# Head pairs in attention: keys and values as 64-row halves in place of a zero-padded block diagonal, with two buffers for the strided values

## The chip, the cores and the metric

The kernel runs on one core of a Trainium2 chip. A core has five engines that run their own instruction streams and meet through semaphores: PE (TensorE, matmuls; its weight loads are listed apart as PEld), DVE (VectorE), ACT (ScalarE), POOL (GpSimd) and SP, which here only issues transfers (DMAs). Matmuls write to PSUM, which has eight banks of 512 f32 values in each of 128 partitions; everything else lives in SBUF, which has 128 partitions (rows) too. The metric is the device time of one execution in microseconds, and the median of several runs counts.

## The reference

An attention layer with 8 heads of 64 values over 8 sequences of 576 positions, and behind it a layer in which each of the 4608 tokens goes to one of 8 experts. The change touches the attention alone.

```python
def _attn_ref(q, k, v):
    B, H, S, D = q.shape                       # 8, 8, 576, 64
    scores = np.matmul(q, k.transpose(0, 1, 3, 2)) / np.sqrt(D)
    rel = pos[:, None] - pos[None, :]
    mask_local = (rel >= 0) & (rel < 32)
    mask_strided = (rel >= 0) & (pos[None, :] % 32 == pos[:, None] % 32)
    masks = np.stack([mask_local if h < H // 2 else mask_strided for h in range(H)], axis=0)
    scores = np.where(masks[None, :, :, :], scores, -1000000000.0)
    scores = scores - np.max(scores, axis=-1, keepdims=True)
    attn = np.exp(scores)
    attn = attn / (np.sum(attn, axis=-1, keepdims=True) + 1e-09)
    return np.matmul(attn, v)

x = attention.transpose(0, 2, 1, 3).reshape(4608, 512)
# per token: e = argmax(x @ w_gate); y = relu(x @ w1[e]) @ w2[e], scaled by two gates
```

Four heads are local (a query sees the 32 positions up to itself), four are strided (it sees the earlier positions of its residue modulo 32).

## The kernel before

**Pairs.** Heads are worked on in pairs: `i` counts the two pairs of a kind, `h` the two heads of a pair. Head `h` of a pair holds its 64 values of depth on rows `64h` to `64h + 63`, so one transfer of queries fills 128 rows with two heads (`q_t`). A query block of one pair is then the 128-row stationary operand of one matmul. So that the two heads don't mix, the moving operand is a block diagonal: the key tiles `kbs` (strided) and `kbl` (local) have an extra dimension `h`, and head `h`'s keys stand on its own 64 rows at place `h`, with zeros on the other 64 rows. One matmul of `scores` gives 64 scores of head 0 and 64 of head 1 beside each other. The value tiles `vlt` (local), `vev` (local, shifted by half a block) and `vst` (strided) are block diagonals in the same way, and one matmul of `values` gives 2 x 65 columns (64 values and a column of ones that sums the weights). The zeros are written once by `clear`, at the program's start, by DVE, POOL and ACT. Each half is loaded by a transfer of its own over 64 partitions (`load_s`, `load_l`, `load_v`); of `vst`, which holds three residues of 18 positions per block, 54 of 64 rows are loaded after the first time.

**Query blocks.** `tiles(j, w)` lists what is computed side by side in one 128-row output: four local blocks of 32 queries, or two strided blocks of 64. A sequence has ten such outputs, two (`w`) in each of five steps `j`: `j` = 0 and 1 are all strided, 2 is mixed, 3 and 4 are all local. A step has 8 (strided), 10 (mixed) or 16 (local) matmuls in `scores` and as many in `values`. Every f32 matmul stands in the trace as two matmul records and two weight loads, so these are groups of 16, 20 and 32 records.

**The pipeline.** The order is written out by hand: a loop over `t` = 0 to 39 (`b = t // 5`, `j = t % 5`), and in each pass parts of several steps: `scores(t)`; the three parts of `norm(t - 4)`; `turn_p(t - 2)` (transposes of the weights, PE); `bar(t)` (mask added, DVE); `evac_p(t - 2)` (ACT); `values(t - 3)` (PE); `top(t)` (row maxima, DVE); `shift(t)` (POOL); `expo(t)` (ACT); `turn_x(t - 4)` (PE); and between them, by `pump`, pieces of the routing of an earlier sequence. Each engine works its stream in this order. The output of `scores` is one bank of PSUM out of two buffers (`ps_s`, `bufs=2`); that of `values` is two banks, one buffer.

**SP's queue.** All loads and the 16 stores of a sequence's rows (`rows`) are issued by SP in program order: among the stores come, at `j` = 1, the strided values of the sequence at work (`vst`, one buffer); at `j` = 2 the strided queries and keys of the next sequence; at `j` = 3 its local queries, keys and values (two buffers each). A transfer is given one of eight semaphores in turn, and SP waits until the earlier transfer of the same semaphore has landed. `vst` can be loaded only when `values` of step `j` = 2 of the sequence before has read it, which runs at `j` = 0; it is needed by `values` of step 0, which runs at `j` = 3.

**Behind the attention** the last sequence is routed, its tokens are sorted into a table in DRAM, and `experts` gathers and multiplies. The first of its work for expert 0 (`lead_layer`) fills the last steps of the attention and uses `scores`' PSUM buffers.

Of the kernel before, what the change touches and what calls it, by code (L numbers as in the profile page):

```python
# [7 lines left out]
F32 = mybir.dt.float32  # L8
# [4 lines left out]
ALU = mybir.AluOpType  # L13
# [10 lines left out]
FC = FF // 128  # L24
# [30 lines left out]
def attn_moe_kernel(  # L55
# [106 lines left out]
    def attention():  # L162
        with ExitStack() as actx:
# [7 lines left out]
            ps_s = actx.enter_context(tc.tile_pool(name="ps_s", bufs=2, space=PSUM))  # L171
# [10 lines left out]
            def clear(t, spare=False):  # L182
                if spare:
                    for ps, h in ((slice(0, D), 1), (slice(D, 128), 0)):
                        dims = " ".join("abcd"[:len(t.shape) - 2])
                        o = t[ps, h].rearrange(f"p {dims} -> p ({dims})")
                        nc.scalar.copy(out=o, in_=zeros[ps, 0:1].to_broadcast([D, o.shape[1]]))
                else:
                    nc.vector.memset(t[0:D, 1], 0.0)
                    nc.gpsimd.memset(t[D:128, 0], 0.0)  # L190
                if t in kbl:
                    nc.vector.memset(t[0:D, 0, :, 0, HS:HS + 32], 0.0)
                    nc.gpsimd.memset(t[D:128, 1, :, 0, HS:HS + 32], 0.0)
                if t is vev:
                    nc.vector.memset(t[32:D, 0, 0], 0.0)
                    nc.gpsimd.memset(t[D + 32:128, 1, 0], 0.0)
# [3 lines left out]
            def load_s(b, cs=slice(0, WS)):  # L200
                if b not in qts:
                    qts[b] = inp.tile([128, 4, WS], F32, name="q_t")
                nc.sync.dma_start(out=qts[b][:, srd, cs], in_=qs[b, :, :, cs])
                for h in range(2):
                    hp = slice(D * h, D * (h + 1))
                    nc.sync.dma_start(out=kbs[b % 2][hp, h, :, cs], in_=ks[b, hp, :, cs])

            def load_l(b, c0=0, c1=HS):
                nc.sync.dma_start(out=qts[b][:, loc, 2 * c0:2 * c1], in_=ql[b, :, :, 2 * c0:2 * c1])
                for h in range(2):  # L210
                    hp = slice(D * h, D * (h + 1))
                    nc.sync.dma_start(out=kbl[b % 2][hp, h, :, :, c0:c1], in_=kl[b, hp, :, :, c0:c1])
# [10 lines left out]
            def load_v(b, t, src, n):  # L223
                for h in range(2):
                    nc.sync.dma_start(out=t[D * h:D * h + n, h], in_=src[b, D * h:D * h + n])

            def even(b, eng, h, f):
# [3 lines left out]
                copy(out=vev[ps, h, f:NL].rearrange("p n i e -> p (n i e)"),  # L231
                     in_=vlt[b % 2][ps, h, 0:NL - f].rearrange("p n i e -> p (n i e)"))
# [13 lines left out]
            def query(b, i, m, n):  # L246
                return qts[b][:, i, 32 * n:32 * (n + 1)] if m == 32 else qts[b][:, 2 + i, col0(n):col0(n) + m]

            def keys(b, i, m, n):

                if m == 64:
                    return kbs[b % 2][:, :, i, col0(n):col0(n) + 64]
                e = n // 2
                step = (HS + 32 if n % 2 else HS) // 32
                kb = kbl[b % 2][:, :, i].rearrange("p h f (n k) -> p h (f n) k", k=32)
# [754 lines left out]
```

## Time and profile before

| | |
|---|---|
| median of 3 runs | 720.11 us (719.47 to 724.35) |
| the profiled execution | 726.38 us, of which its span is 724.7 us |
| PE busy | 671.4 us (93%) |
| DVE, ACT, POOL busy | 310.6, 272.0, 193.6 us |
| mean granted TensorE clock | 0.959 |
| from the first instruction to the first of `scores` | 6.1 us |
| `scores` of `t` = 5 begins | at 26.41 us |
| `scores` of `t` = 39 begins | at 208.74 us |
| the expert layer's long run of matmuls | from 262 us to the end |

The times in the table and in the rows further down are microseconds from the span's start. "Busy" is the time in which at least one instruction of the engine runs; matmuls overlap each other, and their ends are modelled, so the step from the first matmul of one group to the first of the next is the better measure of what a group costs. A wait is named by what released it. The granted clock is the share of full speed that PE was given, and the DMA share is the mean busy share of the core's 16 DMA engines.

### The profile page before, as it was taken

The numbers are of one execution on the slowest core, as the hardware profiler recorded it, in microseconds if no ns is written. First come the engines' busy times: TensorE is split into PE (matmuls) and PEld (weight loads), VectorE is DVE, ScalarE is ACT, GpSimd is POOL, SyncE is SP. The second block draws the span as 40 slices with busy tenths as digits, with TensorE's granted clock in tenths as the row PEclk, the third lists the DMA queues.
The fourth block names the chain that finished last, engine by engine and source line by source line (L and its number), as shares of the span: only waits on it lengthen the run. The fifth ranks groups of instructions, "written<-read, shape, count | busy, mean of one in ns | idle before, by whom it ended". The sixth has DMA issues, their size and how long they took to land.

```text
span 724.7 us, 13154 instructions
## 1 busy us (share of the span) xinstructions
PE 671.4 (93%) x5109; PEld 552.3 (76%) x5109; DVE 310.6 (43%) x670; ACT 272.0 (38%) x491; POOL 193.6 (27%) x197
## 2 busy tenths in 40 slices
PE   7978987988866889999999999999999999999995
PEld 4656655656644678889879987988987997997984
DVE  3766755757643552334223331423543433442410
ACT  6544543544342342333323233423423433432420
POOL 4323452454542343140113012101401302301001
PEclk9999988989998989999999999999999999999998
DMA  8896697687932226362144123424514514531001
GB/s 210 216 228 186 160 212 167 159 214 207 218 100 68 96 69 211 108 192 95 64 142 139 59 102 101 145 72 130 167 35 137 166 56 129 161 101 59 15 13 38
DMA packets 46099, 93.22 MB, mean 129 GB/s; under 512 B 8218, under 2 KB 23066, under 8 KB 46036
## 3 DMA queue, kind: packets, MB, share of 16 engines
q1 hardware_dynamic: 36868, 69.44, 35.7%
q0 software_dynamic: 8048, 19.78, 8.1%
q10 hardware_dynamic: 1120, 3.15, 1.2%
q8 instruction: 41, 0.67, 0.4%
q14 instruction: 22, 0.18, 0.1%
HBM read 73.19 MB, written 20.00 MB: 129 GB/s over the span
## 4 chain that ended last, share of the span: by engine, by line
PE 43%; issue 19%; POOL 3%; DMA 1%; POOLq 0%
PE yp L782 21%; PE hp L766 20%; POOL out_dram L799 2%; PE tp L756 2%; POOL xg L147 1%; DMA xg<-xd,tab 1%; POOL table L554 0%; POOLq L799 0%; POOLq L884 0%; POOLq L147 0%
## 5 line engine op out<-in xcount | busy, mean ns | idle before, releaser
L766 PE MATMUL hp<-xh,w1l 128*128 128x256 f32 (+1 forms) x480 | 147.9, 308 | 0.0
L766 PE MATMUL hp<-xl,w1h 128*128 128x256 f32 (+1 forms) x480 | 147.8, 308 | 0.0
L766 PE MATMUL hp<-xh,w1h 128*128 128x256 f32 (+1 forms) x480 | 147.7, 308 | 0.0
L799 POOL DMA_INDIRECT out_dram<-ys,tab x40 | 41.9, 1048 | 353.2 <-ACT ys L798 341.9
L766 PEld LDWEIGHTS hp<-xh,w1h 128*128 128x128 f32 x480 | 91.0, 190 | 2.1
L766 PEld LDWEIGHTS hp<-xl,w1h 128*128 128x128 f32 x480 | 91.0, 190 | 1.9
L766 PEld LDWEIGHTS hp<-xh,w1l 128*128 128x128 f32 x480 | 90.9, 189 | 1.4
L782 PE MATMUL yp<-w2h,hhb 128*128 128x512 f32 (+3 forms) x208 | 83.8, 403 | 0.0
L782 PE MATMUL yp<-w2l,hhb 128*128 128x512 f32 (+3 forms) x208 | 82.2, 395 | 0.0
L782 PE MATMUL yp<-w2h,hlb 128*128 128x512 f32 (+3 forms) x208 | 81.7, 393 | 0.0
L285 POOL TENSOR_TENSOR p_t<-p_t,st 128x512 f32<-128x512 f32 x40 | 48.1, 1203 | 115.0 <-DVE st L281 73.8
L704 DVE TENSOR_TENSOR xl<-tp,xh 128x512 fp32r<-128x512 f32 (+3 forms) x40 | 25.8, 650 | 118.3 <-ACT xh L703 118.3
L770 DVE SCALAR_TENSOR_TENSOR hlb<-hp,hhb 128x480 fp32r<-128x480 f32 (+7 forms) x64 | 34.6, 541 | 85.7 <-ACT hhb L769 72.7
L703 ACT CAST xh<-tp 128x512 fp32r<-128x512 f32 (+3 forms) x40 | 21.9, 555 | 127.9 <-PE tp L756 127.9
L769 ACT ACTIVATE hhb<-hp 128x480 fp32r<-128x480 f32 (+7 forms) x64 | 30.6, 478 | 101.6 <-PE hp L766 92.1
L314 PE MATMUL xp<-vst,pt 128*64 128x130 f32 x352 | 35.4, 322 | 23.5 <-DMA vst<-in_vs_dram 19.2
L782 PE MATMUL yp<-w2h,hha 128*128 128x512 f32 x128 | 51.9, 405 | 2.3 <-ACT w2h L703 2.3
L782 PE MATMUL yp<-w2l,hha 128*128 128x512 f32 x128 | 51.6, 403 | 0.5 <-DVE w2l L704 0.5
L147 POOL DMA_INDIRECT xg<-xd,tab x40 | 46.6, 1166 | 19.3 <-issue 17.7
L554 POOL DMA_INDIRECT table<-meta,dst x48 | 44.3, 923 | 27.5 <-issue 11.5
L782 PE MATMUL yp<-w2h,hla 128*128 128x512 f32 x128 | 51.1, 399 | 0.0
L314 PEld LDWEIGHTS xp<-vst,pt 128*64 128x64 f32 x352 | 24.6, 157 | 31.3 <-issue 30.3
(148 smaller groups left out, 1110.6 us busy)
## 6 DMA issues: line engine op xcount, KB each, us to landing
raw<-in_moe_w_dram SPq DMA_DIRECT2D x54, 512.0 KB
vlt<-in_vl_dram SPq DMA_DIRECT2D x16, 292.5 KB
q_t<-in_ql_dram SPq DMA_DIRECT2D x8, 576.0 KB
kbl<-in_kl_dram SPq DMA_DIRECT2D x16, 288.0 KB
xd<-x_t SPq DMA_DIRECT2D x80, 54.0 KB
vst<-in_vs_dram SPq DMA_DIRECT2D x14, 301.6 KB
q_t<-in_qs_dram SPq DMA_DIRECT2D x7, 586.0 KB
kbs<-in_ks_dram SPq DMA_DIRECT2D x14, 293.0 KB
```

The source lines that it names most:

```text
L147: nc.gpsimd.indirect_dma_start(out=dst, out_offset=None, in_=src, in_offset=bass.IndirectOffsetOnAxis(ap=idx, axis=0), bounds_check=top, o ...
L285: nc.gpsimd.tensor_tensor(out=p_[b, j], in0=p_[b, j], in1=sp_.pop((b, j)).unsqueeze(3).to_broadcast([128, 2, 4, 64]), op=ALU.subtract)
L314: nc.tensor.matmul(out=xp[p0:p0 + m, w, 130 * i:130 * (i + 1)], lhsT=pt[:, w, i, p0:p0 + m], rhs=value(b, i, m, n), start=True, stop=True)
L554: i = nc.gpsimd.indirect_dma_start(out=table[:, :], out_offset=bass.IndirectOffsetOnAxis(ap=dst[:, j:j + 1], axis=0), in_=meta[:, b * NB + ...
L703: nc.scalar.copy(out=hi, in_=src)
L704: nc.vector.tensor_tensor(out=lo, in0=src, in1=f32(hi), op=ALU.subtract)
L756: nc.tensor.transpose(out=tv[:, k, 0:m], in_=xg[0:m, 128 * k:128 * (k + 1)], identity=ident[0:m, 0:m])
L766: nc.tensor.matmul(out=hp[:, 0:n], lhsT=w[:, k, 128 * j:128 * (j + 1)], rhs=x[:, k, 0:n], start=first, stop=(k == KC - 1 and w is w1l))
L769: nc.scalar.activation(out=hh[:, j, 0:n], in_=hp[:, 0:n], func=AF.Relu)
L770: nc.vector.scalar_tensor_tensor(out=hl[:, j, 0:n], in0=hp[:, 0:n], scalar=0.0, in1=f32(hh[:, j, 0:n]), op0=ALU.max, op1=ALU.subtract)
L782: nc.tensor.matmul(out=yp[0:m, :], lhsT=h[:, j, o:o + m], rhs=w[:, j, :], start=(j == 0 and q == 0), stop=(j == FC - 1 and q == 2))
L799: i = nc.gpsimd.indirect_dma_start(out=out[:, :], out_offset=bass.IndirectOffsetOnAxis(ap=tab[:, 0:1], axis=0), in_=ys[0:m, :], in_offset= ...
```

## The change

The block diagonals go. Keys and values lose the dimension `h` and stand on 128 rows as they come from DRAM, each kind loaded by one transfer over 128 partitions. A matmul now takes 64 rows, the upper or the lower half, of queries and keys (or of weights and values): twice as many matmuls, each with half the rows and half the columns (64 in place of 128, 65 in place of 130). The two heads of a pair come one behind the other and write to different PSUM banks: the tile `sp` of `scores` now has two banks, one for each `h`, and one buffer in place of two (`bufs=1`); in `xp` of `values` the two banks, before one for each `w`, are now one for each `h`. `bar` and `norm` read this other arrangement and write the old one; in the mixed step `bar` is two instructions, since the two `w` have different masks. `vst` has two buffers, and the next sequence's strided values are loaded at `j` = 1, whole (64 rows), in place of those of the sequence at work. The local keys come padded from DRAM (320 in place of 288 columns for each parity), so no zeros are written but 2 x 32 rows of one block of `vev`. `lead_layer` takes one tile of two banks and uses its halves in turn.

```diff
-            ps_s = actx.enter_context(tc.tile_pool(name="ps_s", bufs=2, space=PSUM))
+            ps_s = actx.enter_context(tc.tile_pool(name="ps_s", bufs=1, space=PSUM))
...
-            kbs = [kv.tile([128, 2, 2, WS], F32, name=f"kbs{i}") for i in range(2)]
-            kbl = [kv.tile([128, 2, 2, 2, HS + 32], F32, name=f"kbl{i}") for i in range(2)]
-            vlt = [kv.tile([128, 2, NL, 2, D + 1], F32, name=f"vlt{i}") for i in range(2)]
-            vev = kv.tile([128, 2, NL, 2, D + 1], F32, name="vev")
-            vst = kv.tile([128, 2, NG, 2, D + 1], F32, name="vst")
+            kbs = [kv.tile([128, 2, WS], F32, name=f"kbs{i}") for i in range(2)]
+            kbl = [kv.tile([128, 2, 2, HS + 32], F32, name=f"kbl{i}") for i in range(2)]
+            vlt = [kv.tile([128, NL, 2, D + 1], F32, name=f"vlt{i}") for i in range(2)]
+            vst = [kv.tile([128, NG, 2, D + 1], F32, name=f"vst{i}") for i in range(2)]
+            vev = kv.tile([128, NL, 2, D + 1], F32, name="vev")
...
-                for h in range(2):
-                    hp = slice(D * h, D * (h + 1))
-                    nc.sync.dma_start(out=kbs[b % 2][hp, h, :, cs], in_=ks[b, hp, :, cs])
+                nc.sync.dma_start(out=kbs[b % 2][:, :, cs], in_=ks[b, :, :, cs])
...
-            def load_v(b, t, src, n):
-                for h in range(2):
-                    nc.sync.dma_start(out=t[D * h:D * h + n, h], in_=src[b, D * h:D * h + n])
+            def load_v(b, ts, src):
+                nc.sync.dma_start(out=ts[b % 2], in_=src[b])
...
+            half = lambda h: slice(D * h, D * (h + 1))
+            def packed(j, w):
+                return [(i, p0, m, n, h) for i in range(2) for p0, m, n in tiles(j, w) for h in range(2)]
...
             def scores(b, j):
-                sp = ps_s.tile([128, 2, 4, 64], F32, name="sp")
+                sp = ps_s.tile([128, 2, 512], F32, name="sp")
+                sv = sp[:, :, 0:256].rearrange("p h (w i k) -> p h w i k", w=2, i=2)
                 for w in range(2):
-                    for i in range(2):
-                        for p0, m, n in tiles(j, w):
-                            nc.tensor.matmul(
-                                out=sp[p0:p0 + m, w, 2 * i:2 * i + 2, :].rearrange("p h k -> p (h k)"),
-                                lhsT=query(b, i, m, n), rhs=keys(b, i, m, n), start=True, stop=True)
+                    for i, p0, m, n, h in packed(j, w):
+                        nc.tensor.matmul(out=sv[p0:p0 + m, h, w, i, :], lhsT=query(b, i, h, m, n),
+                                         rhs=keys(b, i, h, m, n), start=True, stop=True)
...
+                for ws in ((slice(0, 1), slice(1, 2)) if j == 2 else (slice(0, 2),)):
+                    nc.vector.tensor_tensor(
+                        out=p_t[:, ws].rearrange("p w (i h) k -> p h (w i) k", h=2),
+                        in0=sv[:, :, ws].rearrange("p h w i k -> p h (w i) k"), in1=msk, op=ALU.add)
...
+                    for i, p0, m, n, h in packed(j, w):
+                        nc.tensor.matmul(out=xv[p0:p0 + m, h, w, i, :], lhsT=pt[half(h), w, i, p0:p0 + m],
+                                         rhs=value(b, i, h, m, n), start=True, stop=True)
...
-            clear(kbs[0])
-            clear(kbl[0])
-            for t in (vlt[0], vev, kbs[1], kbl[1]):
-                clear(t, spare=True)
+            for h in range(2):
+                nc.vector.memset(vev[D * h + 32:D * (h + 1), 0], 0.0)
...
-                if j == 1 and 0 < b < B:
-                    load_v(b, vst, vs, 54)
+                if j == 1 and b + 1 < B:
+                    load_v(b + 1, vst, vs)
```

How the order moves is seen at two places. PE, the step `j` = 3 of the second sequence, from its `scores` to its `turn_x`; `sp`, `tp`, `xp` and `xtp` are the outputs of `scores`, `turn_p`, `values` and `turn_x`, and the brackets name the semaphores waited for (DMAHW: a transfer from SP's queue). Before:

```order
L266 MATMUL sp<-kbl_129,q_t 32x128 x16
L298 MATMUL tp<-ident,p_t 128x128 [waits Activation_49]
L298 MATMUL tp<-ident,p_t 128x128 x3
L314 MATMUL xp<-vst,pt 64x130 [waits DMAHW4_49,DMAHW5_49,DVE_49,PE_49]
L314 MATMUL xp<-vst,pt 64x130 x7
L357 MATMUL xtp<-ident,x_t 128x128 [waits Activation_49]
L357 MATMUL xtp<-ident,x_t 128x128 x3
```

The same place on PE now:

```order
L252 MATMUL sp<-kbl_129,q_t 32x64 [waits DVE_49,PE_49]
L252 MATMUL sp<-kbl_129,q_t 32x64 x31
L288 MATMUL tp<-ident,p_t 128x128 [waits Activation_49]
L288 MATMUL tp<-ident,p_t 128x128 x3
L304 MATMUL xp<-vst_133,pt 64x65 [waits DMAHW1_49,DVE_49,PE_49]
L304 MATMUL xp<-vst_133,pt 64x65 x15
L347 MATMUL xtp<-ident,x_t 128x128 [waits Activation_49]
L347 MATMUL xtp<-ident,x_t 128x128 x3
```

No group moved; `scores` and `values` are twice as many instructions, `scores` waits for DVE (the `bar` that read the one buffer), and `values` for one transfer, of an older load. The second place is SP's queue, from the stores of two steps to the loads for the fourth sequence (`_127`, `_129`, `_131` are the buffers of odd sequences; `xd` is the attention's output in DRAM). Before:

```order
L345 DMA xd<-x_t 3x18x256 x8
L225 DMA vst<-in_vs_dram 54x1430 x2
L345 DMA xd<-x_t 3x18x256 x2
L341 DMA xd<-x_t 64x256
L345 DMA xd<-x_t 2x18x256
L203 DMA q_t<-in_qs_dram 128x1172
L206 DMA kbs_127<-in_ks_dram 64x1172 x2
L341 DMA xd<-x_t 128x256 x2
L209 DMA q_t<-in_ql_dram 128x2x576
L212 DMA kbl_129<-in_kl_dram 64x4x288 x2
L225 DMA vlt_131<-in_vl_dram 64x1170 x2
```

The same place in SP's queue now:

```order
L335 DMA xd<-x_t 3x18x256 x8
L204 DMA vst_133<-in_vs_dram 128x1430
L335 DMA xd<-x_t 3x18x256 x2
L331 DMA xd<-x_t 64x256
L335 DMA xd<-x_t 2x18x256
L187 DMA q_t<-in_qs_dram 128x1172
L188 DMA kbs_127<-in_ks_dram 128x1172
L331 DMA xd<-x_t 128x256 x2
L191 DMA q_t<-in_ql_dram 128x2x576
L192 DMA kbl_129<-in_kl_dram 128x1280
L204 DMA vlt_131<-in_vl_dram 128x1170
```

Four pairs of transfers became one each. The load of strided values stands where it stood, but it is that of the sequence after the one at work.

More of the change, by code (lines that the diff above doesn't have):

```diff
@@ L230, in even @@
                 copy = nc.scalar.copy if eng is nc.scalar else eng.tensor_copy
-                copy(out=vev[ps, h, f:NL].rearrange("p n i e -> p (n i e)"),
-                     in_=vlt[b % 2][ps, h, 0:NL - f].rearrange("p n i e -> p (n i e)"))
+                copy(out=vev[ps, f:NL].rearrange("p n i e -> p (n i e)"),
+                     in_=vlt[b % 2][ps, 0:NL - f].rearrange("p n i e -> p (n i e)"))
             loc, srd = slice(0, 2), slice(2, 4)
@@ L251, in keys @@
                 if m == 64:
-                    return kbs[b % 2][:, :, i, col0(n):col0(n) + 64]
+                    return kbs[b % 2][half(h), i, col0(n):col0(n) + 64]
                 e = n // 2
                 step = (HS + 32 if n % 2 else HS) // 32
-                kb = kbl[b % 2][:, :, i].rearrange("p h f (n k) -> p h (f n) k", k=32)
-                return kb[:, :, e:e + step + 1:step, :]
-            def value(b, i, m, n):
-                return (vst if m == 64 else vlt[b % 2] if n % 2 else vev)[:, :, n if m == 64 else n // 2, i, :]
+                kb = kbl[b % 2][half(h), i].rearrange("p f (n k) -> p (f n) k", k=32)
@@ L261, in scores, with value @@
+                return kb[:, e:e + step + 1:step, :]
+            def value(b, i, h, m, n):
+                return (vst[b % 2] if m == 64 else vlt[b % 2] if n % 2 else vev)[half(h), n if m == 64 else n // 2, i, :]
+            def packed(j, w):
+                return [(i, p0, m, n, h) for i in range(2) for p0, m, n in tiles(j, w) for h in range(2)]
             def scores(b, j):
-                sp = ps_s.tile([128, 2, 4, 64], F32, name="sp")
+                sp = ps_s.tile([128, 2, 512], F32, name="sp")
+                sv = sp[:, :, 0:256].rearrange("p h (w i k) -> p h w i k", w=2, i=2)
@@ L271, in bar @@
+                sp_[b, j] = sv
             def bar(b, j):
@@ L310, in values @@
                 xp = ps_x.tile([128, 2, 512], F32, name="xp")
+                xv = xp[:, :, 0:260].rearrange("p h (w i e) -> p h w i e", w=2, i=2)
                 for w in range(2):
[L312 to L316 removed]
+                    for i, p0, m, n, h in packed(j, w):
+                        nc.tensor.matmul(out=xv[p0:p0 + m, h, w, i, :], lhsT=pt[half(h), w, i, p0:p0 + m],
+                                         rhs=value(b, i, h, m, n), start=True, stop=True)
+                xp_[b, j] = xp[:, :, 0:260].rearrange("p h (g e) -> p h g e", g=4)
             def norm(b, j, part):
@@ L642, in attention @@
                 at(expo, 0)
-                if t in clears:
-                    clear(clears[t])
                 if t + 1 < len(WARM):
```

58 lines of the change are left out of this document (18 added, 40 removed).

## Prediction

> **What bounds the kernel now.** I read the stages first (busy time of each engine by stretch), then PE's timeline over one sequence, then the waits, then SP's queue. The stretches are cut where `scores` of step `j` = 0 begins, so that one row is one sequence. In a row stand: window, its length, busy time (with instruction count) of PE, PEld, DVE, ACT, POOL, then granted clock, DMA share, GB/s.
>
> ```profile
> 0.00:26.41 26.41, 20.24 (x183) 14.27 (x183) 13.54 (x22) 16.99 (x18) 11.48 (x20) 0.94 0.90 217
> 26.41:51.22 24.81, 21.25 (x291) 14.75 (x291) 15.51 (x32) 12.07 (x24) 6.89 (x6) 0.93 0.86 219
> 75.46:102.38 26.92, 22.57 (x306) 15.99 (x302) 16.62 (x48) 12.22 (x26) 11.61 (x12) 0.87 0.76 180
> 102.38:129.70 27.32, 22.75 (x305) 16.10 (x301) 17.04 (x48) 12.23 (x26) 11.62 (x12) 0.88 0.77 178
> 129.70:156.44 26.74, 23.50 (x306) 16.51 (x302) 17.61 (x54) 12.31 (x26) 11.60 (x12) 0.87 0.77 193
> 156.44:181.18 24.74, 22.31 (x305) 15.62 (x301) 17.44 (x48) 12.10 (x26) 12.22 (x13) 0.93 0.73 194
> 181.18:208.74 27.56, 20.68 (x247) 14.98 (x246) 14.89 (x41) 10.66 (x24) 12.38 (x13) 0.88 0.77 195
> 208.74:245.40 36.66, 29.45 (x271) 21.69 (x264) 17.81 (x84) 10.95 (x29) 14.39 (x15) 0.91 0.30 91
> 300.00:400.00 100.00, 100.00 (x551) 87.00 (x550) 34.98 (x49) 34.80 (x58) 22.41 (x29) 1.00 0.38 123
> ```
>
> Six sequences take 181.18 - 26.41 = 154.8 us, 25.8 each. In the expert layer (last row) PE is busy throughout at full clock, and the change touches nothing there: whatever the attention gains or loses arrives at the end. Inside a sequence PE has most busy time, and idles some 4 us. Where is seen in PE's timeline (start, length, what, count of records, idle time before it and its releaser):
>
> ```profile
> 115.29 1.08 PE L266 MATMUL sp<-kbl,q_t 128*32 128x128 f32 x32
> 116.30 0.66 PE L298 MATMUL tp<-ident,p_t 128*128 128x128 f32 x4
> 121.29 2.00 PE L314 MATMUL xp<-vst,pt 128*64 128x130 f32 x16 [4.33 <-DMA vst<-in_vs_dram]
> 123.22 1.11 PE L357 MATMUL xtp<-ident,x_t 128*128 128x128 f32 x4
> 124.27 1.19 PE L389 MATMUL gp<-xt,wgt 128*32 128x288 f32 x8
> 125.23 1.37 PE L266 MATMUL sp<-kbl,q_t 128*32 128x128 f32 x32
> 127.45 1.12 PE L314 MATMUL xp<-vst,pt 128*64 128x130 f32 x16
> 128.49 0.66 PE L357 MATMUL xtp<-ident,x_t 128*128 128x128 f32 x4
> 129.08 0.69 PE L389 MATMUL gp<-xt,wgt 128*32 128x288 f32 x8
> 129.70 1.10 PE L266 MATMUL sp<-kbs,q_t 128*64 128x128 f32 x16
> 130.73 0.44 PE L298 MATMUL tp<-ident,p_t 128*128 128x128 f32 x2
> ```
>
> The step at 115.29 takes 9.94 us, the one at 125.23 takes 4.47. In the first, `values` waits 4.33 us for `vst`; elsewhere one group follows the other. So the attention is bound by PE's stream, and once per sequence by one load. SP's queue shows why it is late:
>
> ```profile
> 112.78 0.76 SPq L225 DMA_DIRECT2D vst<-in_vs_dram  x2
> 116.67 0.81 SPq L203 DMA_DIRECT2D q_t<-in_qs_dram  x1
> 117.53 1.76 SPq L206 DMA_DIRECT2D kbs<-in_ks_dram  x2
> PE xp L314 <- DMA vst<-in_vs_dram: 19.2, 5, 4.4
> PE xp L314 <- DVE vev L231: 4.1, 2, 2.2
> ```
>
> It is issued at 112.78, behind eight stores, 4.1 us before PE could use it (116.30 + 0.6 for the transposes), and has landed 4.3 us after that. The last two rows are PE's waits over the attention (sum, times, longest). I take both as the same wait: seven sequences load `vst` late, and 5 + 2 is seven; where the copy to `vev` is named, it was the last of several conditions.
>
> **Part 1: the wait for `vst`.** With two buffers the load is for the next sequence and has seven steps, some 28 us, to land, against about 4 us before. I cost this wait at nothing afterwards: 19.2 + 4.1 = 23.3 us go. The idle PE also lost clock. In the step at 115.29 the groups after the wait took 2.00, 1.11, 1.19 and 1.37 us; the same groups took 1.12, 0.66, 0.69 and 1.08 otherwise: 2.1 us. Four of the rows above have a clock of 0.87 or 0.88 where the others have 0.93: 4 x 2.1 = 8.4. Together -32 us. (At least the 23.3; at most 5.5 a step, 38.)
>
> **Part 2: PE's groups.** By steps from start to start, a local group takes 116.30 - 115.29 = 1.01 us for 32 records, a strided one 130.73 - 129.70 = 1.03 for 16. The mixed one:
>
> ```profile
> 110.81 0.66 PE L266 MATMUL sp<-kbs,q_t 128*64 128x128 f32 x8
> 112.81 0.66 PE L298 MATMUL tp<-ident,p_t 128*128 128x128 f32 x4
> ```
>
> It takes 2.00, in five pieces. A change of the output's width costs some 0.2 us of this each time, and there are as many changes as before. What is left of a strided group, 0.83 us, is 16 records on two column halves: 0.104 us a record. Halving the columns halves that to 0.052; if upper and lower rows work beside each other, the double number of records runs on four places, and the group is 0.42 + 0.2: -0.41. In a local group the same sum gives 64 / 8 x 0.052 + 0.2 = 0.62, if 64 pairs of weight load and matmul can be fed that fast. How fast PE is fed shows where its queue had run dry:
>
> ```profile
> 137.16 0.11 PEld L314 LDWEIGHTS xp<-vlt,pt 128*32 128x32 f32 x1 [0.26 <-issue]
> 137.25 0.11 PEld L314 LDWEIGHTS xp<-vlt,pt 128*32 128x32 f32 x1
> ```
>
> From the first to the second eight loads start, 13 ns apart, each with its matmul. 64 pairs at 13 ns are 0.83 us, no gain at all for a local group; what the queue took in during the transposes before it goes faster. Between 0 and -0.39 I take -0.2. The mixed group has five pieces of which each loses half of its moving time: -0.5 of 2.00. A sequence has four strided groups, four local and two mixed (`scores` and `values` alike): -1.64 - 0.8 - 1.0 = -3.4 us. From 26.41 to 208.74 there are 34 steps, 6.8 sequences: -23. Ends: no gain (the halves take turns), -29 (all at the ideal), and above zero the first rival.
>
> A rule of the Trainium skill speaks against this part ("TensorE: Matmul & The Clock Gate", section "LDWEIGHTS (loading the stationary operand)"): a weight load takes its columns divided by 1.2 per ns whatever its number of rows, so half-height loads cost as much as whole ones and their number doubles. By it 32 columns are 27 ns, and if loads don't overlap, a local group would be 64 x 27 = 1.7 us in place of 1.01. The trace disagrees in one place, shown with the first rival.
>
> **Part 3: what the faster groups run into.** Without the wait a sequence is 182.3 - 32 = 150.3 us / 6.8 = 22.1; less 3.4 is 18.7. DVE has 17.0 to 17.6 us of work in a sequence, hidden so far. Its work stays (`bar` in the mixed step is two instructions of half the size, 0.1 to 0.7 us, hidden beside PE). One buffer for `scores` makes `scores(t + 1)`, and all PE work queued behind it, wait for `bar(t)`:
>
> ```profile
> L274 DVE TENSOR_TENSOR p_t<-sp,mask 128x512 f32<-128x512 f32 x40 | 27.6, 690 | 43.6 <-PE sp L266 33.2 <-PE tp L298 7.0 <-remote 2.5
> vst<-in_vs_dram SPq DMA_DIRECT2D x14, 301.6 KB
> kbl<-in_kl_dram SPq DMA_DIRECT2D x16, 288.0 KB
> 9.24 2.52 ACT L187 COPY kbl<-xe 64x1280 f32<-64x1280 f32 x2
> ```
>
> `bar` takes 0.69 us and mostly waits for `scores`, so it ends some 1.5 us after the group begins, and a step is near 4: no cost while DVE is not late itself. DMA: 178 GB/s over 27.3 us is 4.86 MB a sequence. Strided values become 64 rows for 54 (301.6 KB x 2 x 10/54 = +112 KB), local keys 320 columns for 288 (+64 KB): 5.04 MB. At full share the rows give 178/0.77 = 231 GB/s in the attention, with half-height loads, and 123/0.38 = 324 in the expert layer, where the weights come over 128 rows. That makes 21.8 or 15.6 us a sequence. SP issues ten loads as six, at about 0.5 us each. I take 20.0 us a sequence: PE's 18.7 and 1.3 given back to DVE and to loads that come just too late. The next late one is the strided pair `q_t` and `kbs`: issued at 116.67 and 117.53, used at 129.70, with the `vst` wait between. Given back: 1.3 x 6.8 = +9 (0 to +21, at 21.8).
>
> **Part 4: the ends.** The eight copies of zeros on ACT end at 11.76 (last row above) and go, as do those of DVE and POOL. But the head is bound by loads (share 0.90), which grow by some 0.2 MB and become full-height: -2, between +1 and -5. Behind 208.74 two steps' `values` get shorter, within that.
>
> **Sum.** 724.7 - 32 - 23 + 9 - 2 = 676.7 us of span. The profiled execution took 726.38 in all, 6.3 above the median of the runs, so the median becomes 720.1 - 48 = 672.
>
> **Rivals.**
>
> *Weight loads or issue bound PE: slower.* If the loads of a group follow one another, twice as many take twice as long: +0.83 for eight groups, +1.0 for two, +8.6 us a sequence, +58 in all; 720 - 32 + 58 - 2 = 744. From +0.47 us a group this eats part 1. For it: a local group's 0.83 us is 26 ns a load, a strided one's 52, in step with the columns, which fits loads as well as moving columns. Against it: loads of 96 columns follow faster than that.
>
> ```profile
> 86.18 0.19 PE L517 MATMUL gp<-ohb,tri 96*96 96x48 bf16 x1
> 86.56 0.30 PE L314 MATMUL xp<-vev,pt 128*32 128x130 f32 x1
> ```
>
> Between these rows lie seven pairs of 96 columns, 53 ns each with the change of width; at 26 ns for 32 columns they would take 78. They are bf16, so it isn't settled. By the skill's rule they would be 80: the trace is below it.
>
> *The halves take turns: the groups stay.* Part 2 is zero, a sequence 22.1 us: 720 - 32 - 2 = 686.
>
> *A load takes the wait's place.* At 231 GB/s, or with `q_t` and `kbs` landing 2 to 3 us after PE wants them, a sequence is 21.8 to 23 us: 684 to 693. For it: DMA share 0.73 to 0.86 already, and the three steps from issue to use shrink. Against it: 324 GB/s with full-height loads.
>
> *The gain is eaten:* groups grow by about 0.47 us, and the time stays within 1%.
>
> **Chances.** The forecast (18 to 21 us a sequence, 658 to 679) 0.56; groups unchanged 0.18; a load bounds 0.14; weights or issue, slower 0.08; eaten 0.04. Faster by over 1% (about what a measurement of this kernel tells from no change) is 0.56 + 0.18 + 0.14 = 0.88, same 0.04, slower 0.08. The range leaves out the last two and a little at each end: low is DVE's 17.3 us a sequence (-65, so 720 - 65 - 3 = 652), high is 700, the load case with the head's loads growing too.
>
> **What would show it.** Part 1: no wait of `values` for `vst`, and a clock near 0.93 in all rows. Part 2: strided groups of 0.6 us, local ones of 0.8, from start to start. Part 3: DVE at 85% or more of a sequence, PE waiting for `bar` or for `x_t`, a DMA rate at full share above 231. I am wrong if local groups exceed 1.2 us, if PE's idle time named "issue" grows past 2 us a sequence, or if `scores` of step 0 waits for `q_t` or `kbs`.

## The result, and the profile after

The changed kernel takes 691.32 us (median of 4 runs, 689.21 to 695.5) where the kernel before took 720.04 beside it: a ratio of 0.960, 95% interval 0.954 to 0.965. It is faster; the forecast was 672 with a range of 652 to 700. The profiled execution took 689.21, with a span of 687.4.

First some stages of the changed kernel, cut as before where `scores` of step 0 begins (window, its length, busy time of PE, PEld, DVE, ACT, POOL, then clock, DMA share, GB/s). Five sequences, from 44.79 to 162.65, take 117.9 us, 23.6 each; before, five took 130.0.

```profile
0.00:23.11 23.11, 17.73 (x330) 13.18 (x330) 9.87 (x19) 6.68 (x10) 7.45 (x14) 0.85 0.91 324
23.11:44.79 21.68, 18.27 (x524) 13.33 (x523) 15.57 (x33) 12.81 (x25) 6.28 (x6) 0.92 0.78 267
67.65:94.14 26.49, 19.77 (x538) 14.19 (x534) 16.58 (x46) 12.09 (x26) 10.97 (x12) 0.87 0.64 195
94.14:117.77 23.63, 18.62 (x538) 13.36 (x534) 18.15 (x52) 12.64 (x28) 12.80 (x13) 0.94 0.77 205
117.77:139.15 21.38, 19.04 (x539) 14.10 (x535) 17.87 (x54) 11.92 (x28) 11.71 (x12) 0.90 0.75 237
139.15:162.65 23.50, 19.07 (x538) 13.84 (x534) 16.38 (x47) 11.38 (x25) 11.33 (x12) 0.93 0.79 254
180.70:215.00 34.30, 27.98 (x412) 20.49 (x409) 21.75 (x88) 15.09 (x35) 18.25 (x20) 1.00 0.38 98
```

PE's busy time in a sequence fell from some 22.5 us to 19, yet some 4.5 us of a row stay idle, and DVE, the next engine, is busy for no more than 18.2 us of a row. What PE waits for, over the attention (sum, times, longest):

```profile
PE sp L252 <- issue: 12.1, 9, 5.9
PE xp L304 <- issue: 10.0, 6, 3.6
PE gp L388 <- ACT lg L383: 5.0, 6, 1.3
PE xtp L347 <- issue: 2.2, 2, 1.7
...
PE sp L252 <- DVE p_t L264: 0.4, 1, 0.4
```

The wait for `vst` is gone, and so is every wait for a load. The single buffer of `scores` costs 0.4 us (last row). In the place of the waits stands "issue", 24.3 us in which PE waited for nothing that the profile shows (before, 2.4 us were named so). The row of `gp` is the routing's own wait for ACT. The longest stop, in PE's timeline:

```profile
78.49 0.73 PE L252 MATMUL sp<-kbl,q_t 64*32 64x64 f32 x49
85.12 0.47 PE L252 MATMUL sp<-kbl,q_t 64*32 64x64 f32 x15 [5.90 <-issue]
85.52 1.11 PE L288 MATMUL tp<-ident,p_t 128*128 128x128 f32 x4
86.56 1.15 PE L304 MATMUL xp<-vst,pt 64*64 64x65 f32 x32
128.08 0.86 PE L252 MATMUL sp<-kbl,q_t 64*32 64x64 f32 x64
128.87 0.66 PE L288 MATMUL tp<-ident,p_t 128*128 128x128 f32 x4
```

PE stops in the middle of a group, after 49 of 64 matmuls whose operands are all there, and goes on 5.9 us later, at about half speed (`tp` 1.11 us against 0.66). What was missing is its program. The page of DMA queues has a queue that loads instructions; its packets are of 16 KB, before (first row) and after:

```profile
q8 instruction: 41, 0.67, 0.4%
q8 instruction: 55, 0.90, 0.6%
```

If all of PE's executed instructions are counted (weight loads, matmuls, and those that wait for semaphores), ten of its eleven stops named "issue" over 0.5 us between 15 and 215 us lie at instruction 449 or a multiple of 256 further on. 256 instructions are one packet at 64 bytes each. Some of these places, from the trace's records (us):

```
block before   fetch packet    PE stops .. goes on   idle    load in flight
 54.1           57.9- 58.9      57.21 ..  60.30       3.10    53.7- 60.8 q_t, kbs (strided)
 76.4           82.4- 83.7      79.00 ..  85.12       6.11    76.4- 83.2 q_t, kbs (strided)
106.9          111.1-112.1     110.37 .. 113.46       3.09    103.6-111.8 q_t, kbs (strided)
119.8          120.5-122.1     (no stop)              0.00    none
149.3          153.6-154.5     152.13 .. 155.95       3.82    147.6-155.0 q_t, kbs (strided)
```

"Block before" is when PE began the block before: in these rows the next one is fetched only after that. Without loads in flight its packet starts 0.7 us later (mostly 1 to 2 us in the run without loads below) and takes 0.9 to 1.6 us; where PE stood still, it went on 1.3 to 1.5 us after the packet had landed. With loads in flight the packet starts only while the last of them lands, 4 to 6 us after PE began the block before. A block lasted 11.4 us on average before (16 blocks between 26.41 and 208.74) and hid this: counted from the same place, the steps across its boundaries add up to 0.7 us. After the change a block lasts 5.4 us (29 blocks between 23.11 and 180.72), and the stops at block boundaries add up to 26.3 us. (Some expectations below start from 5 us for the kernel before. That sum holds 4.2 us of two waits for `vst`, which end at 43.26 and 173.22.)

The Trainium skill knows these blocks ("Runtime: NRT & Kernel Launch", section "Instruction fetch mechanics"): 16 KiB, 256 instructions, the next one fetched by a queue of the engine's own while the current one runs. The trace agrees. It also calls the cost of crossing a boundary "mostly hidden"; here it isn't, by 26.3 us.

### The profile page after: what moved, and what is told of

Read it like the earlier page. It is cut to its first block, busy times and chain, and to the rows that moved or that the text cites. A ratio compares the mean times of both kernels' runs of the same rounds, so it can differ in the third digit from the quotient of the medians.

```text
span 687.4 us, 16812 instructions
## 1 busy us (share of the span) xinstructions
PE 639.0 (93%) x6965; PEld 533.6 (78%) x6965; DVE 306.5 (45%) x673; ACT 260.8 (38%) x483; POOL 187.4 (27%) x190
## 4 chain that ended last, share of the span: by engine, by line
PE 44%; issue 20%; POOL 3%; DMA 0%; POOLq 0%
PE yp L767 22%; PE hp L751 21%; POOL out_dram L784 2%; PE tp L741 2%; POOL xg L147 1%; DMA xg<-xd,tab 0%; POOL table L545 0%; POOLq L784 0%; POOLq L869 0%; POOLq L147 0%
## 5 line engine op out<-in xcount | busy, mean ns | idle before, releaser
L751 PEld LDWEIGHTS hp<-xl,w1h 128*128 128x128 f32 x480 | 91.1, 190 | 1.9
L147 POOL DMA_INDIRECT xg<-xd,tab x40 | 45.3, 1132 | 19.6 <-issue 17.7
L545 POOL DMA_INDIRECT table<-meta,dst x48 | 44.3, 923 | 21.5 <-issue 10.7
L281 ACT ACTIVATE p_t<-p_t 128x512 f32<-128x512 f32 x40 | 25.2, 630 | 62.7 <-POOL p_t L275 62.6
L755 DVE SCALAR_TENSOR_TENSOR hla<-hp,hha 128x256 fp32r<-128x256 f32 x56 | 23.6, 421 | 54.7 <-ACT hha L754 54.7
```

The lines of the kernel that those rows point to most:

```text
L147: nc.gpsimd.indirect_dma_start(out=dst, out_offset=None, in_=src, in_offset=bass.IndirectOffsetOnAxis(ap=idx, axis=0), bounds_check=top, o ...
L281: nc.scalar.activation(out=p_t, in_=p_t, func=AF.Exp, scale=scale)
L545: i = nc.gpsimd.indirect_dma_start(out=table[:, :], out_offset=bass.IndirectOffsetOnAxis(ap=dst[:, j:j + 1], axis=0), in_=meta[:, b * NB + ...
L751: nc.tensor.matmul(out=hp[:, 0:n], lhsT=w[:, k, 128 * j:128 * (j + 1)], rhs=x[:, k, 0:n], start=first, stop=(k == KC - 1 and w is w1l))
L755: nc.vector.scalar_tensor_tensor(out=hl[:, j, 0:n], in0=hp[:, 0:n], scalar=0.0, in1=f32(hh[:, j, 0:n]), op0=ALU.max, op1=ALU.subtract)
```

## The experiments

Theory: PE's faster groups are right, and PE starves for instructions, because it uses up a block sooner than the next one gets through the loads. Rivals: another engine or a load paces the sequence, and the stops only show slack; or the halves of a group don't overlap. And of the forecast's part 1: what removed the wait for `vst`, the second buffer or the loads over 128 rows? All times below of "five sequences" are five whole ones from the third on, "stops" the idle time at block boundaries from the start of the second sequence to the last `scores` (as the 26.3 us above). Both come from one profiled execution each, while executions of one kernel differ by 3 to 10 us. Ratios are to the kernel before in runs on the same chip; the versions ran on several chips, so versions are best compared by their ratios.

| kernel | ratio, 95% interval | five sequences | stops |
|---|---|---|---|
| before | 1 | 130.0 | 0.7 |
| changed | 0.960 (0.954-0.965) | 117.9 | 26.3 |
| no loads | (other routing) | 98.2 | 9.2 |
| loads spread | 0.966 (0.959-0.972) | 118.9 | 26.2 |
| loads in twelve pieces | 0.996 (0.991-1.000) | 124.4 | 16.8 |
| one `vst` | 0.970 (0.965-0.975) | 119.0 | 27.4 |
| half-height loads | 0.988 (0.982-0.993) | 123.4 | 12.4 |
| both of these | 0.996 (0.992-0.999) | 124.8 | 11.6 |
| before, two `vst` | 1.008 (1.004-1.013) | 126.8 | 0.5 |
| before, matmuls doubled | 1.000 (0.997-1.003) | 132.0 | 5.5 |
| halves one after the other | 1.015 (1.007-1.022) | 133.7 | 11.5 |
| local steps block-diagonal | 0.974 (0.967-0.982) | 113.0 | 3.2 |
| the same, two queues | 0.985 (0.979-0.990) | 128.4 | 6.3 |
| local values block-diagonal | 0.956 (0.952-0.960) | 120.3 | 22.9 |

### Without the loads

```diff
-                    load_s(b + 1)
+                    qts[b + 1] = qts[(b + 1) % 2]
-                if j == J_L and b + 1 < B:
+                if j == J_L and b + 1 < 2:
...
-                if j == J_V and b + 1 < B:
+                if j == J_V and b + 1 < 2:
```

> The changed kernel without the loads of queries, keys and values for sequences 2 to 7: their steps compute on what sequences 0 and 1 left in the buffers, so that part of the computation is not the reference's. All instructions of the engines stay. Theory (PE starves for instructions, because the 16 KB blocks of its program wait behind the loads on the same DMA engines): the idle time at block boundaries, 28.3 us before 230 us in the changed kernel, falls below 8, no gap exceeds 1 us, and the time falls by 20 us or more, to 655 to 670, part of it by a better clock. Rival A (fetching a block takes as long by itself, so PE outruns it with or without loads): gaps stay near 0.5 to 1 us at nearly every boundary, 20 us in sum, and the time falls by less than 8. Rival B (another engine paces the sequence and the gaps only show slack): the gaps go, but PE waits for DVE or ACT in their place, and the time stays within 8 us of 691.

Its total, 771.0 us, says nothing: the gates are computed from other values, and the expert layer gets other tokens. In the attention two sequences with no load beside them read

```profile
46.12:64.78 18.66, 17.12 (x538) 12.71 (x534) 17.04 (x49) 11.75 (x27) 7.69 (x8) 1.00 0.22 66
64.78:83.72 18.94, 17.40 (x537) 12.73 (x533) 16.91 (x49) 11.62 (x26) 11.42 (x11) 1.00 0.23 68
```

Same instructions, 23.6 us become 18.7 to 18.9, at full clock. Over five sequences 19.7 us go, and the stops within them fall from 22.1 to 7.4 us, which is 14.7 of the 19.7; the rest goes with the clock (0.98 against 0.91 over the five). DVE, with 17 us, does not hold PE up. So loads cost the changed kernel 4 us a sequence though PE never waits for their data. Two stops above 1 us stayed, so fetching isn't free even without loads: rival A holds for about a third of the stops (7.4 of 22.1 us).

### Loads spread, and loads in pieces

One load at a time in place of bursts:

```diff
-                if j == J_S and 0 < b < B - 1:
-                    load_s(b + 1)
...
+                if j == 0 and 0 < b < B - 1:
+                    qts[b + 1] = inp.tile([128, 4, WS], F32, name="q_t")
+                    nc.sync.dma_start(out=qts[b + 1][:, srd], in_=qs[b + 1])
+                if j == 1 and 0 < b < B - 1:
+                    nc.sync.dma_start(out=kbs[(b + 1) % 2], in_=ks[b + 1])
...
```

> The changed kernel with its six loads for a sequence issued one at a time over the five steps (q_s and k_s at the starts of steps 0 and 1, q_l in step 2, k_l late in step 2, strided values late in step 3, local values late in step 4), so that seldom more than one load is in flight. Theory (a block of instructions waits behind the loads in flight): the gaps at block boundaries fall from 28.3 us to 10 to 18, none above 2.5 us, and the time falls by 8 to 18 us, to 673 to 683. Rival A (fetch time by itself): gaps unchanged, the time within 3 us of the changed kernel's. Rival C (loads now land late): PE waits for q_t, kbs or kbl, some 1 to 3 us a sequence, and the time rises.

A miss: nothing changed. A single load takes 4 us too (stores run beside it), and a fetch asked for in that time starts as it ends: the local values land from 66.7 to 71.0 and the packet starts at 71.3; from 138.4 to 142.8, and at 143.0. Rows of the next load move from 69.2 and from 141.4 on, so the packet seems to wait for what was queued before it, not for the queue to be empty. The number of loads in flight wasn't the matter; one is enough.

Then each load in two pieces, by columns, at twelve places:

```diff
+                piece(b, 3 * j)
                 at(scores, 0)
...
+                piece(b, 3 * j + 1)
                 at(bar, 0)
...
+                piece(b, 3 * j + 2)
                 at(top, 0)
```

> The changed kernel with each of its six loads for a sequence cut into two column halves over all 128 partitions, the twelve pieces issued one by one at three places of each step (start, after the stores, before the row maximum), in steps 0 to 3. With whole loads issued one at a time the fetch of a block began as the load in flight ended, 3 to 4.7 us after the block before it had begun. Theory (the block waits for what is queued on its DMA engine when it is asked for): a piece is over in 1.5 to 2 us, so the wait halves, gaps at block boundaries over five sequences fall from 22 us to 8 to 14, and the time falls by 6 to 14 us against the changed kernel, to 0.942 to 0.952 of the time of before. Rival (what counts is the DMA engines' total share, not the size of a burst): gaps and time as in the changed kernel, 0.957 to 0.967.

The stops within five sequences fell from 22.1 to 13.3 us, as the theory has it, and the kernel still became slower by 6.5 us in these five and by some 26 in all (by the ratios). Other pauses of PE took their place, of 0.5 to 0.9 us, in mid-group and not at block boundaries (28 between 46 and 215 us, 18.1 us; 3 in the changed kernel). The section on the hardware shows them, and why they may belong to the chip that this version ran on. So smaller bursts do shorten the stops; whether the time would follow without the pauses stays open.

### What removed the wait for `vst`

```diff
-            vst = [kv.tile([128, NG, 2, D + 1], F32, name=f"vst{i}") for i in range(2)]
+            vst = [kv.tile([128, NG, 2, D + 1], F32, name="vst0")] * 2
...
-                if j == 1 and b + 1 < B:
-                    load_v(b + 1, vst, vs)
+                if j == 1 and 0 < b < B:
+                    load_v(b, vst, vs)
```

> The changed kernel with one buffer for the strided values, loaded at step 1 of the sequence that uses it, as in the kernel before. Prediction's part 1: the wait of values for vst comes back, 3 to 4 us in each of seven sequences, with colder groups behind it, 20 to 32 us, so 711 to 723. Theory of instruction fetch adds: while PE waits for vst its next block of instructions arrives, so part of the wait is not lost on top; gaps at block boundaries fall by 4 to 10 us, and the net loss is 12 to 22 us: 703 to 713. If the full-height load over 128 rows lands much sooner than the half-height ones did, the loss is below 8 us.

With one buffer again, as before, PE waits for `vst` nowhere; the loss is 3 us by the medians and 7 by the ratios. The last row of the load over 128 rows lands 5.8 us after its issue (101.06 to 106.8), in time for `values` at 109.65; before it took 7.5 (112.78 to 120.3). The larger difference is that SP issues the load earlier: from issue to the end of the transposes before `values` it has 8 us and more in every later sequence, where it had 4 to 5 in most before. The other side, height taken away and two buffers kept:

```diff
-                nc.sync.dma_start(out=kbl[b % 2], in_=kl[b])
+                for hp in (slice(0, D), slice(D, 128)):
+                    nc.sync.dma_start(out=kbl[b % 2][hp], in_=kl[b, hp])
...
```

> The changed kernel with the loads of strided keys, local keys, strided values and local values each issued as two of 64 rows, as in the kernel before; buffers and all engine instructions stay. If height is what made the loads faster (full share moves 340 to 356 GB/s in the changed kernel against 231 before), the share rises to above 0.9, a sequence takes at least 21 to 22 us by DMA, blocks of instructions wait longer, and the time rises by 8 to 20 us. If loads are hidden and the blocks wait by bytes in flight alone, the time stays within 4 us of the changed kernel's.

The keys and values of the other kinds are cut in the same way. It costs 17 us by the medians, 20 by the ratios, and PE's list of waits names the next late load:

```profile
PE sp L255 <- DMA kbs<-in_ks_dram: 21.3, 13, 3.5
PE xp L307 <- issue: 6.6, 4, 2.1
```

In the trace's packets a row of local keys (5120 bytes) takes 196 ns in the median over 128 rows and 378 as halves; of local values (4680 bytes) 181 and 308. Half the rows cost 1.7 to 1.9 times the time a byte. The Trainium skill says why ("SBUF — State Buffer", section "Door 1: The DMA port swizzle"): 64 rows reach 8 of the 16 ports. Its section "Can I just issue two DMAs to hit both halves?" adds that two transfers to the two halves don't make up for it. The trace agrees, with 181 ns against 308. The forecast had the two rates from its rows, but let neither the wait nor its end hang on them. Both edits together leave PE's part of the change, almost alone (the strided values keep all 64 rows, the local keys their padding):

> The changed kernel with the loads of keys and values in 64-row halves and one buffer for the strided values, loaded for the sequence at work: only the change to PE's matmuls (row halves) is left. With two buffers half-height loads cost 16 us and made scores wait 21 us for kbs; with full-height loads one buffer cost 3 us. If PE's faster groups (prediction's part 2, 23 us) are worth something by themselves, 0.965 to 0.975 of before. If half-height loads bound both kernels, the waits move to vst and kbs and take most of it: 0.985 to 1.005.

The faster groups are worth 0.4% by themselves. The wait for `vst` is back, and takes what PE gains:

```profile
PE xp L307 <- DMA vst<-in_vs_dram: 20.3, 12, 4.4
```

This kernel and the one with one `vst` differ in the height of the loads alone, and in that the wait is there or gone. So the height did it, not the buffer. In ratios, one part after the other: PE's halves 0.996, with the loads over 128 rows 0.970, with the second buffer 0.960. The second buffer in the kernel before, the forecast's part 1 alone:

```diff
+            vst = [kv.tile([128, 2, NG, 2, D + 1], F32, name=f"vst{i}") for i in range(2)]
...
+                if j == 1 and b + 1 < B:
+                    load_v(b + 1, vst[(b + 1) % 2], vs, 54 if b else D)
```

> The kernel before with a second buffer for the strided values, loaded a sequence ahead (room for it is made by 3 buffers in place of 8 for gathered rows of the expert layer, which starts after the attention). Part 1 of the prediction alone: the wait of values for vst, 23 us, goes, and colder groups with it: 32 us less in the attention, five sequences in 107 to 110 us where before took 130. Rival (another load takes its place, since 64-row loads keep the DMA engines at a share of 0.8): scores waits for kbs or q_t, the five sequences take 118 us or more, and less than half of the 32 us is gained.

```profile
PE sp L266 <- DMA kbs<-in_ks_dram: 20.8, 6, 5.0
```

The 23.3 us of waiting for `vst` became 20.8 of waiting for `kbs`; five sequences gained 3.2 us in place of 20 and more, and the whole stretch up to the last `scores` 9.3 us (182.3 to 173.0), most of it behind the five sequences. The ratio of 1.008 also holds 8.9 us that the time behind the last `scores` grew, where the fewer buffers are; that they caused it is not shown.

### Instructions and halves

Before's kernel with as many PE instructions as after:

```diff
+                            for h in range(2):
+                                nc.tensor.matmul(out=sp[p0:p0 + m, w, 2 * i + h, :], lhsT=query(b, i, m, n),
+                                                 rhs=keys(b, i, m, n)[:, h], start=True, stop=True)
...
```

> The kernel before with each matmul of scores and values cut in two, one head's columns each, both over all 128 rows: as many PE instructions as in the changed kernel, on the loads, buffers and block-diagonal operands of the kernel before. If a weight load or the issue of a pair costs what its columns say (27 ns, rival of the prediction), local groups go from 1.0 to 1.7 us: 40 us or more, 1.055 and up. If pairs are fed at 13 to 15 ns, the groups stay at 1.0 to 1.1 us, since the moving columns are the same in sum. Theory of starved instructions: blocks then last about 6 us, gaps at block boundaries before 230 us rise from 5 to 12 to 25 us, part of it hidden by the waits for loads: 1.005 to 1.03. Rival (instruction count does not matter, the gaps of the changed kernel are due to the row halves): gaps stay near 5 us, 0.995 to 1.005.

Its groups, and a strided one of the changed kernel with the row behind it:

```profile
111.20 1.20 PE L267 MATMUL sp<-kbs,q_t 128*64 128x64 f32 x32
112.33 0.66 PE L298 MATMUL tp<-ident,p_t 128*128 128x128 f32 x4
```

```profile
121.60 0.69 PE L252 MATMUL sp<-kbs,q_t 64*64 64x64 f32 x32
122.22 0.66 PE L288 MATMUL tp<-ident,p_t 128*128 128x128 f32 x4
```

32 pairs of 64 columns take 1.13 us over all rows and 0.62 on halves: upper and lower rows do work beside each other. That a matmul of 64 rows might simply be quicker is ruled out by the single records: over all rows two matmuls start close together and the next two 58 ns later (111.304, 111.363, 111.421 us for the first of each two); on halves four start within 20 ns, and the next four again 58 ns later (121.704, 121.762, 121.821). 64 pairs of a local group took 1.12 us (112.91 to 114.03), so a pair costs at most 17.5 ns, whatever its weight load. The stops rose from 0.7 to 5.5 us, at a block that lasts 6.4 us, so matmuls over all rows meet them too (1.42 us at 30.40, 1.21 at 37.71, 1.23 at 163.40). That is far less than the theory asked for, and the time did not move, as the rival had it. PE still waits 21.5 us for `vst`, and blocks can arrive meanwhile; that this is why the stops are few is argued, not shown.

Fewer instructions with the loads kept: block diagonals put back in the two local steps, `for h` gone from their matmuls, their operands loaded in halves.

```diff
+                if j > 2:
+                    for w in range(2):
+                        for i in range(2):
+                            for p0, m, n in tiles(j, w):
+                                nc.tensor.matmul(out=sp[p0:p0 + m, w, 128 * i:128 * (i + 1)],
...
```

> The changed kernel with the block-diagonal form put back for the two purely local steps of a sequence (their keys and values padded with zeros again and loaded in 64-row halves), strided and mixed steps on row halves as changed. PE gets 256 instructions, one block, fewer a sequence, and its local groups take 1.0 us in place of 0.8. Theory of starved instructions: PE 0.8 us a sequence slower, gaps over five sequences from 22 us to 10 to 14; the half-height local loads cost up to 1 us a sequence; net between 4 us slower and 8 faster than the changed kernel, 0.95 to 0.966 of before. Rival (gaps only show slack, PE's stream is what counts): 5 to 12 us slower, 0.967 to 0.977.

A block lasts 7.1 us, and the stops are nearly gone: 3.2 us, of them 1.8 in one, with as many bytes loaded and at a worse rate. Five sequences take 113.0 us although their local groups are slower and `scores` waits 6.4 us for `kbs`. Part of the drop may lie in these waits: the version with half-height loads and all of the instructions has stops of 12.4 us, where the changed kernel has 26.3. The step from 12.4 to 3.2 fits the smaller count of instructions. The total is worse: behind the last `scores` this kernel takes 516.2 us, as the kernel before did (516.0), and the changed one 506.7. The block diagonals are not the reason, since the kernel with the matmuls doubled has them too and takes 508.5; over all versions but the one without loads this stretch lies between 505 and 525 us, and what sets it was not tried.

```profile
46.74:159.70 112.96, 95.53 (x2030) 70.27 (x2027) 85.87 (x247) 60.91 (x134) 54.82 (x54) 0.95 0.77 219
```

Two attempts to keep this gain. Lower halves loaded by ACT's queue beside SP's upper ones:

> As the version with block-diagonal local steps, with the lower 64 rows of local keys and local values loaded by a queue of ACT at the same time as SP loads the upper ones. If a half-height load is slow because its packets all go to one half of the rows, both together run at the full-height rate, scores stops waiting for kbs (6.4 us before) and the five sequences fall from 113 to 107 us or less: 6 to 10 us faster than that version, 0.96 to 0.967 of before. If the rate is bound otherwise, within 3 us of it, 0.97 to 0.978.

It failed, as the second section of the skill named above has it: the packets stayed slow (340 ns in the median for 5120 bytes), the wait for `kbs` grew to 14.4 us, and five sequences took 128.4. And block diagonals for the local values only, whose load has nothing behind it:

> The changed kernel with block-diagonal local values alone in the two purely local steps (their values padded and loaded in two 64-row halves; local keys and everything strided as changed): half a block of PE instructions fewer a sequence, and the half-height load is the last of a sequence, with nothing queued behind it. With both local operands block-diagonal the gaps at block boundaries were gone, 5 sequences took 113 us in place of 118, but scores waited 6 us for kbs. Theory of starved instructions: gaps between 23 and 181 us fall from 26 us to 8 to 15, no wait for kbs, 5 sequences in 110 to 114 us, 4 to 8 us faster than the changed kernel: 0.948 to 0.956 of before. Rival (the half-height load costs as much as the gaps did): 0.957 to 0.975.

The stops hardly fell (22.9 us, in an execution that was the slowest of six) at a block of 6.2 us, and the time can't be told from the changed kernel's: the intervals overlap. No version tried beats the changed kernel beyond its uncertainty.

Last, the order within a group:

```diff
-                return [(i, p0, m, n, h) for i in range(2) for p0, m, n in tiles(j, w) for h in range(2)]
+                return [(i, p0, m, n, h) for h in range(2) for i in range(2) for p0, m, n in tiles(j, w)]
```

> The changed kernel with the matmuls of a group in another order: all of the upper rows' first, then all of the lower rows'. Same instructions, same loads. If neighbours on upper and lower rows work beside each other, that is lost: the strided group goes from 0.63 to about 1.0 us from start to start, the local one from 0.8 to about 1.0, a sequence by 3 us, 20 us in all without anything else. Theory of starved instructions: a block of 256 then lasts 0.6 us longer and waits as much less, gaps over five sequences fall from 22 us to 10 to 14, and the net loss is 8 to 13 us: 0.971 to 0.979 of before. If the gaps do not answer, 0.985 to 0.992. If the halves never overlapped, groups and time stay as they are, 0.957 to 0.965.

This tells less than it was made for. At full clock a strided group takes 0.67 us, against 0.62: in this order, too, the halves change after every four matmuls of a strided output, and rows that wait for each other hardly show. The kernel also has the pauses that struck the twelve pieces, and a clock of 0.71 in one sequence; what the order costs can't be told from these.

## Why the prediction was right, and where it was off

**Direction and range** held. The median moved by -28.7 us where -48 was forecast. The spans of the two profiled executions differ by more, -37.3, because that of the kernel before ran 6.3 us above its median and that of the changed one 2.1 below: -3.3 up to the first whole sequence (forecast -2), -24.7 in the 6.8 sequences (forecast -32 - 23 + 9 = -46), and -9.3 behind the last `scores` (forecast nothing). That the time stayed in the range was in part luck: the upper end of 700 had been set for loads that come late, and no load did; what came in their place had no price.

**Part 1** saw the wait for `vst` go, and it went; its cause was put in the wrong place. The second buffer is worth 3 to 7 us in the changed kernel and 9 in the attention of the one before; the wait moves to `kbs` if the loads stay half as high. The rival "a load takes the wait's place" was right for the buffer alone.

**Part 2** was right in each size: 0.62 us for a strided group (forecast 0.62), 0.79 for a local one (128.08 to 128.87; forecast 0.8), 1.41 for the mixed one (forecast 1.5). The sequence of 18.7 us that follows from them is what the kernel without loads comes near: 18.66 and 18.94 in the two rows above, 19.6 in the mean of five, with stops of 1.5 in each. The rival by the Trainium skill's rule on weight loads fell: by it a local group would have been 1.7 us.

**Part 3 is the step that was mis-sized**: "+9 (0 to +21)" given back to DVE and late loads. Given back were 30 us (32 + 23 - 24.7), more than its upper end, and to something else: DVE hides beside PE at 17 us, no load is late, and 26.3 us are stops for instructions, with slow groups after the long ones. The forecast had named this as a sign of being wrong ("PE's idle time named 'issue' grows past 2 us a sequence": it is 3.9 in the five whole sequences). By that sign its account of what a faster PE runs into was wrong. No price stood on it, though twice the instructions were counted. The rows to price it from were on the page before: 41 instruction packets, and a block each 11 us.

**Part 4** was right for the head. The 9.3 us behind the last `scores` come with a clock of 1.00 in the row from 180.70, where before had 0.91. They need not be an effect of the change: the kernel before with its matmuls doubled takes 508.5 us there, in place of 516.0. What sets this stretch was not tried.

## What to carry to other kernels

Count PE's instructions when a change splits matmuls, and set the time of 256 of them against what a fetch takes while loads are in flight: here blocks of 11.4 us lost 0.7 us in all, blocks of 7.1 lost 3.2, and blocks of 5.4 lost 26.3. When a wait for a load goes, ask why that load was late before crediting the buffer: the height of the transfers moved 17 to 20 us here, the buffer 3 to 9. And try each part of a change alone: PE's part gave 0.4% by itself, since another limit stood right behind it.

## What the runs showed of the hardware

Besides the instruction blocks: in two kernels (halves one after the other, loads in pieces) PE advances in small jumps while SP issues the four strided stores of a step. PE's timeline of the first, then SP's:

```profile
122.21 0.79 PE L252 MATMUL sp<-kbl,q_t 64*32 64x64 f32 x40
123.41 0.33 PE L252 MATMUL sp<-kbl,q_t 64*32 64x64 f32 x5 [0.41 <-issue]
124.17 0.32 PE L252 MATMUL sp<-kbl,q_t 64*32 64x64 f32 x4 [0.43 <-issue]
124.93 0.46 PE L252 MATMUL sp<-kbl,q_t 64*32 64x64 f32 x15 [0.45 <-issue]
```

```profile
122.28 2.85 SPq L335 DMA_DIRECT2D xd<-x_t  x4
```

Four issues of 0.7 us, and beside them pauses of 0.65 us from one start to the next (0.41 to 0.45 of it idle). Of 23 such pauses 16 lie over four fifths within such issues (16 of 28 with the pieces), though these issues fill only some 30% of the time. The changed kernel has the same stores and 3 such pauses. The version with block-diagonal local steps has 9, of which at most 3 lie in an issue. All three ran on one chip, on which no other version of the experiments with row halves ran. So the pauses, and with them part of the time that these three lose, may belong to that chip and not to the kernels; this stays open.

The clock falls in or after a long stop. In the trace's record of the granted clock, the stops of 1.9 to 3.8 us that end at 38.84, 60.30, 113.46, 134.04 and 155.95 are each followed within 1.6 us by 3.4 us at 0.5 of full speed. Around the longest stop, which ends at 85.12, the clock is at 0.5 from 84.3 to 91.1, so PE works at half speed for 6 us (four transposes take 1.11 us at 85.52 and at 87.64, and 0.66 at 91.39). In the kernel with the halves one after the other it stays at 0.5 for 17 us, from 103.9 to 121.0 (0.71 over that sequence). None of the pauses of 0.65 us lies in that stretch; what kept the clock low there is not known.
